# The order table of a fused RWKV-6 and Hyena kernel, searched anew

## The chip, the cores and the metric

The kernel runs on one core of a Trainium2 chip. The core has five engines that each work through a queue of their own in order: TensorE (PE, whose weight loads are shown apart as PEld), VectorE (DVE), ScalarE (ACT), GpSimd (POOL) and SyncE (SP, which here only issues DMAs). The metric is the device time of one execution in microseconds, lower is better; the time before is a median of 3 runs.

## The reference, cut to what matters

Two stages. The first is a recurrence over 768 time steps for each of 4 batches and 8 heads of width 48; the second takes its output as 4 sequences of 768 tokens and 384 channels.

```python
def _attn_ref(r, k, v, w, u):                 # each [4, 8, 768, 48]
    for t in range(S):
        cur = np.einsum('bhd,bhe->bhde', u[None] * kt, vt)
        y[:, :, t] = np.einsum('bhd,bhde->bhe', rt, state + cur)
        state = wt[:, :, :, None] * state + np.einsum('bhd,bhe->bhde', kt, vt)

def _moe_ref(x, w_proj, filter_fft, w_out):   # x [4, 768, 384]
    x1, x2, x3 = split(x @ w_proj)
    x2_conv = np.fft.irfft(np.fft.rfft(x2, axis=1) * np.fft.rfft(filter_fft, axis=0)[None], axis=1)
    return (x1 * x2_conv * x3) @ w_out
```

## The kernel before, in words

**First stage.** Each sequence of 768 steps is cut into 6 chunks of 128, and two chunks are treated as a pair, so there are 12 pairs (`group(gi, i0)` and `pair(i0, gi)`, with i0 = 0, 2, ... 22). A pair's four inputs come by one 384 KB DMA each: `lw`, `lk`, `lr`, `lv`. Then, for pair number gi and its chunks i:

- `wm` multiplies neighbouring decays, `ln` (ACT) takes the logarithm, `cs` (PE) sums it up, `ex` (ACT) takes the exponential, and `kq` (DVE, one per chunk) scales keys and receptances with it into a bf16 tile `kq`. `tr` (PE) transposes that, `qk` (ACT, one per chunk) evicts it, `sc` (PE) makes the scores.
- The scores are evicted and cut by a mask into the tile `mt`, in one of three ways: one DVE multiplication for both halves (written `M` in the table), one DVE multiplication per half (`mt i.a D`), or an ACT copy (`A`) and a POOL multiplication behind it (`mc i.a G`).
- `rk`, `ru`, `rh`, `cc`, `vc` make the term with u: a product of r and k, times u, an addition of the two halves of each row (`rh`), a sum along the row (`cc`, over 24 elements if `rh` ran and over 48 if it did not, written `M`), and a product with v in bf16 (`vb` is the cast of v).
- `ki` and `kv` (PE) and `su` (DVE) carry the state; `yi`, `ys`, `y` (PE) make the output of the pair, `xn` (ACT) evicts it, `yt` (PE) and `xT` transpose it for the second stage.

**Second stage**, once per batch b, as soon as its 6 chunks are there: `p` and `q` project x to x1 and x3 (L1561) with evictions `cp` and `cq` (`cq` multiplies both), `xw` projects to x2 (L1601) with `cxw`; `sd` adds and subtracts halves of the sequence, `f` is the forward transform as matmuls (L1458) with `cf`; `u`, `p` without numbers of halves (DVE, L1638) multiply with the filter's spectrum; `E` is the inverse transform (L1656), `cE` and `aE` evict it, and `yE` multiplies with the gate. An `E` with the letter `Q` writes a folded form in matmuls of half the width, which two more additions `dE` on DVE or POOL unfold; with `P` there are no such additions. `o` projects out (L1720), `co` evicts, `so` stores. The filter's own spectrum is made once: three DMAs `filt`, two DVE operations `fsd` (L1521), then `h`, `hc`, `hg`.

**Start.** `ang`, `ia` (DVE) and `sin`, `is` (ACT) make the transform's matrices; `if` flips some of them. ACT holds one table of functions at a time; a row `table` loads another.

**What sets the order.** Each operation is registered with `plan.op(...)`, and the string `ORDER` (line 45 on) says line by line which comes next, on which engine, and in which of the 8 PSUM banks it writes. `Plan.run` emits them in that order, so an engine's queue is the sequence of its own rows. Waits between engines follow from the tiles that are read and written. A third word that names a DVE operation is a tie: the instruction waits until that operation has ended. `warm` and `spare` are matmuls on zeros (512 or 128 columns) that fill PE's idle time. A helper records most elementwise work, so many groups of the profile have the lines L1104 (a product) or L1108 (an ACT copy).

```python
            o = self.ops.pop(name)
            if o.one or o.two:
                place[(o.one + o.two)[0]] = int(more[0])
            got = o.fns[e](e, place)
            if more and got is not None and more[0] in last:
                tie(got, last[more[0]])
```

Of the kernel before, what the change touches and what calls it, by code (L numbers as in the profile page):

```python
# [271 lines left out]
wm4 D
vb3 A
yt3 P 2
ru4 D
yt5 P 7
lr10 S
qk6 A
xT3 D
kv6 P  # L280
vc3 G wm4
rh4 -
cc4 M
xT5 A
qk7 A
xw0.4 P 6
lv8 S
cxw0.0 A
su6 D
rk6 D  # L290
ln4 A
sc6 P 4
sc7 P 0
lw10 S
cxw0.4 A
xw0.2 P 2
mt6.0 M
kw6 G su6
cs8 P 6
lr14 S  # L300
cxw0.2 A
mt7.0 M
p0.0.1 P 4
sd0.0.0 D
p0.0.0 P 0
cp0.0.1 A
ru6 D
p0.2.0 P 4
sd0.1.0 D
lk14 S  # L310
cp0.0.0 A
ki7 P 5
q0.0.1 P 2
rk5 D
cp0.2.0 A
lv10 S
ex8 A
rh6 D
kv7 P
cq0.0.1 D  # L320
wm6 G rk5
vb4 A
f0.0 P 0
lw14 S
kq9 D
vc4 G rk5
f0.1 P 2
cf0.0 A
su7 D
kq8 D  # L330
f0.2 P 0
cf0.1 A
wm5 G
lv16 S
cc6 D
tr8 P 2
cf0.2 A
ru5 D
kw5 D
yi6 P 4  # L340
lr16 S
qk9 A
ys7 P
qk8 A
# [7 lines left out]
u10.0 D  # L352
ph8 A
sc8 P 0
lv12 S
xn7 A
q0.0.0 P 6
xn6 A
u00.0 D
mt8.0 N  # L360
lw16 S
ki8 P 3
kv8 P
# [44 lines left out]
vb8 A
cq0.2.1 D
cs12 P 0  # L410
kq11 D
p1.0.0 P 4
ph10 A
cE0.1 A
wm8 G
ex12 A
aE0.1.0 D
lk18 S
tr10 P 6
kw7 G  # L420
aE0.1.1 D
cp1.0.0 A
kq12 D
xw1.0 P 2
qk10 A
vb6 A
kq13 D
q1.0.0 P 4
lw20 S
qk11 A  # L430
vc6 G
rh5 -
cc5 M
lv18 S
ph12 A
cxw1.0 A
tr12 P 6
lr18 S
cq1.0.0 D
sc11 P 0  # L440
qk12 A
p1.2.0 P 2
vc5 G
qk13 A
mt11.0 M
ki10 P 4
kv10 P
cp1.2.0 A
lr20 S
sc10 P 5  # L450
ln8 A
ki12 P 7
mt10.0 M
yt9 P 3
wm9 G
E0.0 Q 0
xT9 A
sc12 P 2
cE0.0 A
rk8 G  # L460
su10 D
kv12 P
yi10 P 5
vb7 A
aE0.0.1 D
ys10 P
ys11 P
mt12.1 D
mt12.0 A
mc10.0 -  # L470
mt10.1 -
mc10.1 -
mc11.0 -
mt11.1 -
mc11.1 -
y10 P
lv22 S
aE0.0.0 D
lv20 S
cs14 P 2  # L480
xn11 A
mc12.0 G
su12 D
xn10 A
sc13 P 0
yt11 P 4
ex14 A
mt13.0 M
yt10 P 5
kw8 G  # L490
E0.2 P 6
xT10 A
xT11 A
# [1322 lines left out]
```

## Time and profile before

| | |
|---|---|
| median of 3 runs | 157.8 us (157.19 to 158.36) |
| the profiled execution | 158.33 us, of which 156.6 us are the span of the profile |
| busy | PE 143.6 us, DVE 143.2, ACT 111.9, POOL 93.0 |
| PE's matmuls on zeros, in the first 60 us | 19.35 us |
| read and written | 22.41 MB and 4.72 MB |

The span runs from the first to the last instruction of the profiled execution. Of the 22.41 MB most are the inputs of the pairs, which are read in the first 85 us. The pairs and the second stage of the batches overlap: the filter's spectrum is made at about 27 to 34 us, the second stage of the first batch starts at about 40 us, and the last 20 us hold the second stage of the last batch alone.

### The profile page before, as it was taken

What the parts mean: (1) busy time and instruction counts of PE and PEld (TensorE: products, weight loads), DVE (VectorE), ACT (ScalarE), POOL (GpSimd) and SP (SyncE); (2) the same over time, 40 slices, a digit from 0 to 9 for tenths busy, and PEclk for the clock granted to TensorE, in tenths of its full rate; (3) what the DMA queues carried; (4) which work ended last, traced back from release to release, by engine and by line L of the source; (5) the groups of instructions that cost most, each with busy time, mean ns of one, the idle gap of its engine ahead of it and who ended that gap; (6) DMA issues with size and microseconds to landing.
All of it is one profiled execution on the core that took longest, in us unless ns stands there. A gap on an engine that the chain in (4) does not pass through costs nothing.

```text
span 156.6 us, 5491 instructions
## 1 busy us (share of the span) xinstructions
PE 143.6 (92%) x2321; PEld 88.3 (56%) x2321; DVE 143.2 (91%) x245; ACT 111.9 (71%) x202; POOL 93.0 (59%) x85
## 2 busy tenths in 40 slices
PE   6888997898999999989999898999999999999990
PEld 2243544465755557547656674676656767556650
DVE  6999999999999999899999899799899997799860
ACT  3595976858787788798787596896764597654561
POOL 6915493659271729959959776793779527400300
PEclk9999999999999999999999999999999999999999
DMA  4999999999999999399797300510000050000665
GB/s 120 315 303 305 272 236 306 374 257 251 284 274 262 285 293 273 102 249 255 189 259 181 60 4 0 207 73 34 0 4 0 4 201 4 0 0 4 249 261 193
DMA packets 53770, 27.19 MB, mean 174 GB/s; under 512 B 50289, under 2 KB 52210, under 8 KB 53746
## 3 DMA queue, kind: packets, MB, share of 16 engines
q1 hardware_dynamic: 53346, 26.55, 59.2%
q0 software_dynamic: 400, 0.29, 1.4%
q8 instruction: 18, 0.29, 0.8%
q14 instruction: 6, 0.05, 0.1%
HBM read 22.41 MB, written 4.72 MB: 173 GB/s over the span
## 4 chain that ended last, share of the span: by engine, by line
PE 55%; DVE 23%; ACT 11%; issue 6%; POOL 2%; ACTq 1%; POOLq 0%; DVEq 0%
PE banks L1561 11%; PE banks L1720 8%; PE banks L1601 7%; PE banks L1458 6%; DVE kq L1287 5%; PE banks L1656 4%; PE banks L1322 3%; DVE P L1521 2%; PE banks L1365 2%; DVE cc L1259 2%; PE banks L1391 2%; PE banks L1400 2%; PE banks L1423 2%; DVE mt L1332 2%; ACT qk L1108 2%
## 5 line engine op out<-in xcount | busy, mean ns | idle before, releaser
L1561 PE MATMUL banks<-xT,wproj 128*128 128x384 bf16 x144 | 28.3, 326 | 0.0
L1332 DVE TENSOR_TENSOR mt<-banks,mask_cut 128x1024 bf16<-128x1024 f32 (+1 forms) x22 | 24.8, 1142 | 0.9 <-PE banks L1322 0.8
L1104 POOL TENSOR_TENSOR vc<-vb,cc 128x768 bf16<-128x768 bf16 x12 | 18.3, 1525 | 10.7 <-ACT vb L1108 7.2
L1108 ACT ACTIVATE x<-banks 128x768 bf16<-128x768 f32 (+1 forms) x28 | 19.6, 714 | 5.8 <-PE banks L1601 3.8
L1287 DVE TENSOR_TENSOR kq<-banks,kr 128x768 bf16<-128x768 f32 x24 | 22.1, 946 | 0.2
L1104 POOL TENSOR_TENSOR kr<-kr,w 128x768 f32<-128x768 f32 x7 | 13.9, 1990 | 6.8 <-DMA w<-in_w_dram 2.1
L1561 PEld LDWEIGHTS <-wproj 128*128 128x128 bf16 x144 | 13.0, 97 | 8.2 <-issue 0.7
L1160 PE MATMUL banks<-wt 128*128 128x512 bf16 x61 | 17.2, 426 | 0.0
L1108 ACT ACTIVATE X<-banks 128x768 bf16<-128x768 f32 x12 | 9.8, 813 | 7.8 <-PE banks L1458 7.7
L1601 PE MATMUL banks<-wproj,xT 128*128 128x384 bf16 x72 | 14.1, 327 | 1.0 <-ACT xT L1108 0.8
L1104 POOL TENSOR_TENSOR rk<-kr 128x768 bf16<-128x768 f32 x7 | 14.3, 2043 | 0.3 <-DVE g L1589 0.2
L1108 ACT ACTIVATE qk<-banks 128x512 f32<-128x512 f32 x24 | 13.6, 602 | 1.3 <-PE banks L1301 1.3
L1104 POOL TENSOR_TENSOR y<-y,g 128x768 bf16<-128x768 bf16 (+1 forms) x5 | 6.7, 1351 | 12.8 <-DVE y L1682 12.4
L1589 DVE TENSOR_TENSOR g<-banks,x 128x768 bf16<-128x768 f32 (+1 forms) x16 | 12.7, 802 | 1.2 <-ACT qk L1108 1.2
L1458 PE MATMUL banks<-sd,F 128*128 128x384 bf16 (+1 forms) x96 | 13.5, 328 | 0.0
L1337 POOL TENSOR_TENSOR mt<-mt,mask_cut 128x512 bf16<-128x512 bf16 (+1 forms) x5 | 7.9, 1590 | 8.9 <-ACT mt L1108 8.9
L1720 PE MATMUL banks<-wout,y 128*128 128x384 bf16 x72 | 13.2, 326 | 0.0
L1108 ACT ACTIVATE xn<-banks 128x384 bf16<-128x384 f32 x24 | 10.6, 492 | 3.5 <-PE banks L1391 3.1
L1104 POOL TENSOR_TENSOR wp<-w 128x384 f32<-128x384 f32 x11 | 11.1, 1006 | 3.2 <-PE banks L1561 3.2
L1108 ACT ACTIVATE o<-banks 128x768 f32<-128x768 f32 (+1 forms) x14 | 9.5, 697 | 4.2 <-PE banks L1720 4.0
L1458 PEld LDWEIGHTS <-F 128*128 128x128 bf16 (+1 forms) x120 | 8.6, 103 | 6.6 <-issue 2.5
L1104 POOL TENSOR_TENSOR rk<-rk,u_b 128x768 bf16<-128x768 bf16 x4 | 6.9, 1736 | 8.6 <-DVE rk L1104 4.9
(115 smaller groups left out, 326.7 us busy)
## 6 DMA issues: line engine op xcount, KB each, us to landing
w<-in_w_dram SPq DMA_DIRECT2D x12, 384.0 KB, 5.1
kr<-in_k_dram SPq DMA_DIRECT2D x12, 384.0 KB, 5.3
kr<-in_r_dram SPq DMA_DIRECT2D x12, 384.0 KB, 5.7
v<-in_v_dram SPq DMA_DIRECT2D x12, 384.0 KB, 5.3
out_dram<-o SPq DMA_DIRECT2D x9, 384.0 KB, 2.8
x<-in_moe_w_proj_dram SPq DMA_DIRECT2D x2, 576.0 KB, 7.3
out_dram<-o SPq DMA_DIRECT2D x6, 192.0 KB, 1.9
U<-in_moe_filter_fft_dram SPq DMA_DIRECT2D x2, 384.0 KB, 7.1
```

The source lines that it names most:

```text
L1104: return eng(e).tensor_mul(o, a, b)
L1108: return nc.scalar.activation(out=o, in_=a, func=AF.Copy)
L1160: nc.tensor.matmul(banks[:, at, :].rearrange("p (a t) -> p a t", a=2), wt[:, 0:L], _mid(wt, 2), start=True, stop=True)
L1287: op(f"kq{i0 + a}", [DVE], lambda e, bk, a=a: nc.vector.tensor_mul(kq[fs[a]][:, :, :, 0:D], csp(bk)[:, :, 0:C].rearrange("p m (h d) -> p m ...
L1332: return copy(ACT, o, x) if e in (ACT, ACT2) else nc.vector.tensor_mul(o, x, _mid(mask_cut[:, c], n))
L1337: return nc.gpsimd.tensor_mul(o, o, _mid(mask_cut[:, c], n))
L1458: nc.tensor.matmul(p[rows], F[:, ti, c0 + rows.start:c0 + rows.stop], x[q][:, ti, :], start=(ti == 0), stop=(ti == NT - 1),)
L1561: nc.tensor.matmul(p, wproj[:, cb, col0:col0 + L], xT[bx][:, cb, sl], start=(cb == 0), stop=(cb == CB - 1),)
L1589: op("c" + n3, [DVE], lambda e, bk: nc.vector.tensor_mul(g[bx][:, fs, sl].rearrange("p f (t a) -> p f a t", a=2), halved(view(bk, n3)), ha ...
L1601: nc.tensor.matmul(view(bk)[:, z], xT[bx][:, cb, (c0 + z) * L:(c0 + z + 1) * L], wproj[:, cb, C:2 * C], start=(cb == 0), stop=(cb == CB - 1),)
L1656: nc.tensor.matmul(o, P[:, q, m, cs], x, start=start, stop=stop)
L1720: nc.tensor.matmul(view(bk)[:, z], yt_[:, z, :], wout[:, cb, :], start=(cb == 0), stop=(cb == CB - 1),)
```

## The change

Only the string `ORDER` is another one; the code that builds operations is the same. The new table has the same operations. Their order differs in nearly every stretch, by a few places mostly, and so do banks. Apart from order and banks it changes these choices (before, then now; `-` means that the operation is left out or done with its neighbour):

```
start       kz1, kz3, rk1: DVE -> POOL      wm1, ru1, rk2: POOL -> DVE
            rh0, rh1: - -> POOL, tied       cc0, cc1: over 48 (M) -> over 24 (D)
            mt0.0, mt0.1: one DVE product (M) -> ACT copy with POOL product mc0.0, and DVE product
            ACT's tables: 4 loads -> 6 loads
to 65 us    mt4: M -> two DVE products      xT3: DVE -> ACT       wproj1: POOL -> ACT
            rh4, cc4: -, M -> D, D          rh6, cc6: D, D -> -, M
            rk5: DVE -> POOL, tied to sd0.1.0
later       mt8: one ACT copy and one POOL product -> two of each
            vb5: ACT -> POOL   rh5: - -> POOL, cc5: M -> D   rk10: POOL -> DVE
            E0.0: Q with dE0.0.0 and dE0.0.1 on POOL -> P
            xT12, xT21, xT23, cp2.2.1, co3.1: DVE -> ACT     cE2.1: ACT -> DVE
            rh9, cc9: -, M -> D, D    rh11: - -> POOL, tied; cc11: M -> D
            mt16: its two halves change engines
            dE1.1.1, yE2.1, yE3.0.0: POOL -> DVE
            dE2.2.0, sd3.1.2, yE3.0.1, yE3.2.1: DVE -> POOL
zero work   warm 61 -> 79 (50 of them ahead of the first tr), spare 15 -> 13
```

Three lines of the diff show the form:

```diff
-rk5 D
+rk5 G sd0.1.0
...
-E0.0 Q 0
+E0.0 P 4
```

**ACT's queue at the start.** Before, from the second table load to the first eviction `qk` of the first pair and on to the logarithm of the third pair (lg is the logarithm's tile, banks the sums of `cs`, F and mi the transform's matrices):

```order
L987 ACT_TABLE_LOAD
L1235 ACTIVATE lg_75<-wp_65 128x8x48
L1235 ACTIVATE lg_74<-wp_64 128x8x48
L1283 ACTIVATE banks<-banks 128x2x384 x2
L1108 ACTIVATE vb_83<-v_70 128x768
L1290 ACTIVATE phi<-banks 128x8
L1108 ACTIVATE qk_96<-banks 128x512
L1108 ACTIVATE qk_95<-banks 128x512
L987 ACT_TABLE_LOAD
L1471 ACTIVATE F<-o_127,mpi 128x768
L1471 ACTIVATE F<-o_128,mpi 128x768
L987 ACT_TABLE_LOAD
```

Now, the same stretch from its second table load to the fifth (mt_99 is the first half of the scores of chunk 0):

```order
L986 ACT_TABLE_LOAD
L1470 ACTIVATE mi<-X,mpi 128x6x192
L986 ACT_TABLE_LOAD
L1282 ACTIVATE banks<-banks 128x2x384
L1234 ACTIVATE lg_75<-wp_65 128x8x48
L1107 ACTIVATE vb_83<-v_70 128x768
L1289 ACTIVATE phi<-banks 128x8
L1107 ACTIVATE qk_96<-banks 128x512
L1107 ACTIVATE qk_95<-banks 128x512
L1234 ACTIVATE lg_76<-wp_64 128x8x48
L1282 ACTIVATE banks<-banks 128x2x384
L986 ACT_TABLE_LOAD
```

Two loads more stand in the queue, around the sine `mi`, which stood ahead of the second load before; the exponential of the second pair (L1282) has moved behind the evictions `qk` of the first.

**DVE ahead of the filter.** Before, from the state of chunk 0 (S_104) to the scores of chunk 3 (P<-U is `fsd`):

```order
L1371 TENSOR_TENSOR S_104<-banks,phi 128x384
L1332 TENSOR_TENSOR mt_99<-banks,mask_cut 128x1024
L1259 TENSOR_REDUCE cc_80<-rk_77 128x16
L1332 TENSOR_TENSOR mt_100<-banks,mask_cut 128x1024
L1371 TENSOR_TENSOR S_105<-banks,phi 128x384
L1521 TENSOR_TENSOR P<-U 128x1152
L1104 TENSOR_TENSOR rk_79<-rk_79,u_b 128x768
L1521 TENSOR_TENSOR P<-U 128x1152
L1332 TENSOR_TENSOR mt_102<-banks,mask_cut 128x1024
L1287 TENSOR_TENSOR kq_91<-banks,kr_68 128x16x48
L1287 TENSOR_TENSOR kq_90<-banks,kr_68 128x16x48
```

Now, the same stretch:

```order
L1370 TENSOR_TENSOR S_104<-banks,phi 128x384
L1286 TENSOR_TENSOR kq_92<-banks,kr_67 128x16x48
L1370 TENSOR_TENSOR S_105<-banks,phi 128x384
L1258 TENSOR_REDUCE cc_81<-rk_78 128x16
L1286 TENSOR_TENSOR kq_93<-banks,kr_67 128x16x48
L1331 TENSOR_TENSOR mt_99<-banks,mask_cut 128x512
L1520 TENSOR_TENSOR P<-U 128x1152 x2
L1103 TENSOR_TENSOR rk_79<-rk_79,u_b 128x768
L1286 TENSOR_TENSOR kq_91<-banks,kr_68 128x16x48
L1286 TENSOR_TENSOR kq_90<-banks,kr_68 128x16x48
L1331 TENSOR_TENSOR mt_102<-banks,mask_cut 128x1024
```

The two `fsd` now follow each other directly, only one half of mt_99 is left on DVE, and the scores of chunk 3 (mt_102) have moved behind the third pair's two `kq`.

**DVE where the first batch's second stage begins** (sd are the sums and differences, g a gate). Before:

```order
L1371 TENSOR_TENSOR S_106<-banks,phi 128x384
L1104 TENSOR_TENSOR rk_77<-kr_68 128x768
L1332 TENSOR_TENSOR mt_101<-banks,mask_cut 128x1024
L1332 TENSOR_TENSOR mt_102<-banks,mask_cut 128x1024
L1612 TENSOR_TENSOR sd<-x_114 128x1152
L1104 TENSOR_TENSOR rk_77<-rk_77,u_b 128x768
L1612 TENSOR_TENSOR sd<-x_114 128x1152
L1104 TENSOR_TENSOR rk_79<-kr_67 128x768
L1256 TENSOR_TENSOR rk_77<-rk_77 128x16x24
L1589 TENSOR_TENSOR g_111<-banks,x_110 128x2x2x192
```

Now:

```order
L1103 TENSOR_TENSOR rk_77<-kr_68 128x768
L1103 TENSOR_TENSOR rk_77<-rk_77,u_b 128x768
L1370 TENSOR_TENSOR S_106<-banks,phi 128x384
L1331 TENSOR_TENSOR mt_101<-banks,mask_cut 128x1024
L1331 TENSOR_TENSOR mt_102<-banks,mask_cut 128x1024
L1611 TENSOR_TENSOR sd<-x_114 128x1152 x2
L1258 TENSOR_REDUCE cc_81<-rk_78 128x16
L1286 TENSOR_TENSOR kq_90<-banks,kr_66 128x16x48
L1370 TENSOR_TENSOR S_103<-banks,phi 128x384
```

The product `rk5` (rk_79<-kr_67) has left DVE's queue for POOL's, the two `sd` stand together, and `cc4` (cc_81) has come in behind them.

1155 lines of the change are left out of this document (577 added, 578 removed).

## The prediction

> **What bounds the kernel now.** The page's first two parts come first: which engine is full, and when.
>
> ```profile
> PE 143.6 (92%) x2321; PEld 88.3 (56%) x2321; DVE 143.2 (91%) x245; ACT 111.9 (71%) x202; POOL 93.0 (59%) x85
> PE   6888997898999999989999898999999999999990
> DVE  6999999999999999899999899799899997799860
> ```
>
> Two engines are full at once. PE's digits of the first third contain matmuls on zeros, so the view of stretches says more (columns: PE, PEld, DVE, ACT, POOL busy, clock, DMA share, GB/s), with the tile of zeros alone beneath.
>
> ```profile
> 4.00:65.00 61.00, 56.06 (x940) 32.50 (x937) 60.32 (x101) 46.19 (x79) 36.66 (x30) 1.00 1.02 281
> 26.80:65.00 38.20, 36.32 (x681) 23.10 (x680) 37.86 (x55) 29.87 (x56) 23.89 (x16) 1.00 1.00 278
> 65.00:150.00 85.00, 82.51 (x1365) 53.51 (x1364) 79.03 (x125) 62.07 (x117) 53.59 (x38) 1.00 0.32 94
> 150.00:156.60 6.60, 2.44 (x15) 1.27 (x13) 1.32 (x3) 2.35 (x5) 0.00 (x0) 1.00 0.66 238
> ...
> 26.80:60.00 33.20, 2.61 (x18) 1.22 (x18) 0.00 (x0) 1.00 1.03 286
> ```
>
> From 4 to 65 us DVE is busy 60.32 of 61 us: there it is the bound. PE has room there: from 26.8 to 65 us 38.2 - 36.32 + 2.61 of zeros = 4.5 us. From 65 to 150 us it turns round: PE idles 85 - 82.51 = 2.49 us, DVE 5.97, and the last 6.6 us are copies and stores. So DVE work taken out before 65 us counts in full, PE work added after 65 us counts in full, DVE work after that counts little.
>
> **Prices.** Groups with shapes apart (out<-in, count, busy us, mean ns):
>
> ```profile
> L1332 DVE TENSOR_TENSOR mt<-banks,mask_cut 128x1024 bf16<-128x1024 f32 x19 | 22.8, 1216 | 0.9 <-PE banks L1322 0.8
> L1332 DVE TENSOR_TENSOR mt<-banks,mask_cut 128x512 bf16<-128x512 f32 x3 | 2.0, 679 | 0.0
> L1259 DVE TENSOR_REDUCE cc<-rk 128x16 f32<-128x768 bf16 x10 | 9.4, 941 | 0.0
> L1259 DVE TENSOR_REDUCE cc<-rk 128x16 f32<-128x384 bf16 x2 | 1.1, 541 | 0.0
> L1256 DVE TENSOR_TENSOR rk<-rk 128x384 bf16<-128x384 bf16 x2 | 0.7, 346 | 0.0
> L1104 DVE TENSOR_TENSOR rk<-kr 128x768 bf16<-128x768 f32 x5 | 4.8, 951 | 0.0
> L1104 DVE TENSOR_TENSOR rk<-rk,u_b 128x768 bf16<-128x768 bf16 x8 | 4.4, 544 | 0.0
> L1104 DVE TENSOR_TENSOR wp<-w 128x384 f32<-128x384 f32 x1 | 0.6, 550 | 0.0
> L1195 DVE MEMSET kq<- 128x128 uint32 x3 | 0.5, 165 | 0.0
> L1110 DVE COPY xT<-banks 128x384 bf16<-128x384 bf16 x4 | 1.4, 350 | 0.2 <-PE banks L1423 0.2
> L987 ACT ACT_TABLE_LOAD x4 | 5.1, 1283 | 0.8 <-PEq L1800 0.8
> L1108 ACT ACTIVATE mt<-banks 128x512 bf16<-128x512 f32 x3 | 1.8, 592 | 0.5 <-PE banks L1322 0.5
> L1656 PE MATMUL banks<-mi,P 128*128 128x384 bf16 x42 | 7.7, 326 | 0.0
> L1656 PE MATMUL banks<-mi,P 128*128 128x192 bf16 x20 | 2.5, 246 | 0.0
> ```
>
> **The start, up to the end of the filter's `fsd`.** DVE loses kz1 and kz3 (2 x 0.165), rk1 (0.951), the full mt0 (1.216) and two long sums cc (2 x 0.941): 4.38 us. It gains ru1 (0.544), wm1 (0.550), rk2 (0.951), half an mt (0.679) and two short sums (2 x 0.541): 3.81. That is 0.57 less. Two more rows count here, and both come from DVE's and POOL's timelines and the list of DMAs (start, us; the last row is the issue whose landing time stands above it):
>
> ```profile
> 9.14 0.96 DVE L1104 TENSOR_TENSOR rk<-kr 128x768 bf16<-128x768 f32 x1
> 22.54 2.52 DVE L1521 TENSOR_TENSOR P<-U 128x1152 bf16<-128x1152 f32 x1
> 25.45 1.35 DVE L1521 TENSOR_TENSOR P<-U 128x1152 bf16<-128x1152 f32 x1
> ...
> 22.37 1.48 POOL L1104 TENSOR_TENSOR vc<-vb,cc 128x768 bf16<-128x768 bf16 x1
> ...
> kr<-in_r_dram SPq DMA_DIRECT2D x1, 384.0 KB, 4.4
> 4.14 0.38 SPq L1229 DMA_DIRECT2D kr<-in_r_dram  x1
> ```
>
> The first fsd takes 2.52 us and the second, of equal size, 1.35. POOL's vc began 0.17 us ahead of the first and ended at 23.85, and the fsd ended 1.2 us later: it stood behind vc. Now vc0 comes earlier and rk3 is tied behind the second fsd, so 1.17 us go. Against that, rk0 needs the load lr0. Before it was the fourth large load and landed at 4.14 + 4.4 = 8.5 us; now it is the fifth. With 281 GB/s in the row of the first stretch, 384 KB take 1.4 us, so it lands at about 9.9 (an estimate), where DVE started rk0 at 9.14: 0.8 us of waiting. DVE would so be 0.57 + 1.17 - 0.8 = 0.9 us early behind the filter.
>
> I do not count it, because of ACT. Chunk 3's scores mt3.0 have moved behind kq4, and they wait for `sc3`, that for `qk2`, and in ACT's queue qk2 now stands behind mt0.0, ex4, both xn, vb1 and xT0; and ACT has two table loads more. The added ACT work is 2 x 1.283 + 0.592 = 3.16 us. What covers it are ACT's own waits there:
>
> ```profile
> 13.84 0.84 ACT L1108 ACTIVATE vb<-v 128x768 bf16<-128x768 f32 x1 [1.14 <-DMA v<-in_v_dram]
> 22.45 0.52 ACT L1235 ACTIVATE lg<-wp 128x384 bf16<-128x384 f32 x1 [1.03 <-POOL wp L1104]
> 25.17 0.49 ACT L1108 ACTIVATE xn<-banks 128x384 bf16<-128x384 f32 x1 [1.16 <-PE banks L1391]
> 28.03 0.81 ACT L1527 ACTIVATE hh<-banks 128x768 bf16<-128x768 f32 x1 [0.93 <-PE banks L1458]
> ```
>
> Together 4.26 us of waiting, so the 3.16 fit, but with little over, and ACT is then full up to qk2. Those 0.9 us are what I expect mt3.0 to wait. **Start: 0**, with the bounds -0.9 (ACT covered) and +2.3 (3.16 bare, less 0.9).
>
> How long a table switch holds ACT is read here:
>
> ```profile
> 8.73 1.28 ACT L987 ACT_TABLE_LOAD   x1
> 10.02 0.94 ACT L1235 ACTIVATE lg<-wp 128x384 bf16<-128x384 f32 x2
> ```
>
> The load ends at 10.01 and the logarithm starts at 10.02. [...]
>
> **From there to 65 us, on DVE.** xT3 goes (0.350), rk5 goes (0.951); mt4 in halves adds 2 x 0.679 - 1.216 = 0.14; rh4 with the short cc4 is 0.346 + 0.541 - 0.941 = -0.05, and cc6 the reverse. **-1.16 us**, on the engine that is the bound, and PE with its 4.5 us of room can follow. rk5 on POOL is tied behind the first sd, and vc4 stands behind it; POOL is busy 36.66 of 61 us there, and its work hides unless yi6 waits for vc4. Between -1.16 and 0 (PE not following) I take all of it: nothing else in that stretch is full.
>
> **After 65 us.** E0.0 without folding: four matmuls of 192 columns become 384, 4 x (326 - 246) = **+0.32 us** on PE, which is the bound there. The two additions dE0.0 leave POOL, where they waited for nothing that PE needs soon. On DVE rk10 comes in (0.951), three xT go (1.05), and cc5 and cc11 get short (0.80); the copies and small products that are swapped with ACT and POOL besides are of about half a microsecond each and more leave than come. That is some 0.9 us less, but DVE has 5.97 us idle there: 0 for the end, and at best all of PE's 2.49 idle us. ACT takes the copies; it is busy 62.07 of 85 us. co3.1 on ACT falls in the last 6.6 us, in which ACT is busy 2.35: 0. The loads have nearly all landed by then (share 0.32). The zeros behind the filter are of about equal number in both tables, and those ahead of it fill PE's waits: 0.
>
> **Sum:** 0 - 1.16 + 0.32 = -0.84 us. The profiled execution took 158.33 us (span 156.6), so 157.5 for it; that execution lies 0.53 above the median of 157.8, so **157.0 us** as a median. A measurement of this kernel can tell about 1%, 1.6 us, from no change: the forecast is within it.
>
> **Rivals.**
>
> *ACT becomes the bound of the start (slower).* One mechanism: the table loads, six now, that stand ahead of the exponentials of the first and third pair. The point from which it decides: qk2's eviction ends after DVE has finished kq4, and PE's y0 and h wait for ACT too. For it: the added 3.16 us against 4.26 of cover, and lr0's later landing moves the whole chain of the first pair. Against: 1.14 of the cover is a wait for lv0, the eighth large load in both tables. Price: 3.16 bare, -0.84 + 3.16 = +2.3, **160.1 us**.
>
> *POOL and DVE block each other more often (slower).* The row of fsd shows the price: 1.17 us for one meeting. POOL newly gets rk1, rh0, rh1, mc0.0, rk5, rh5, rh11, dE2.2.0, sd3.1.2 and a part of yE3. Most of them are tied to the end of a DVE operation, but rk1, mc0.0, rh5 and yE3.0.1 are not. Three meetings on the path: 3.5 - 0.84 = +2.7, **160.5 us**. [...]
>
> *The gain reaches further (faster).* ACT covers the start (-0.9), and PE's waits after 65 us are halved (-1.25), since DVE has 0.9 us less to do there and xT copies no longer stand in its queue: -0.84 - 0.9 - 1.25 = -3.0, **154.8 us**.
>
> *The relief does not arrive (no change).* If PE, not DVE, sets the pace already from 27 us on, the -1.16 are lost and E0.0 costs 0.32: **158.1 us**.
>
> **How the numbers follow.** The forecast 0.30, the relief that does not arrive 0.12: both within 1%, together 0.42. The faster rival 0.28. ACT at the start 0.18, the blocking 0.12: slower, together 0.30. The two tables are the same in structure, and no stretch is rebuilt, which keeps the ends near. The range leaves out the outer half of the faster rival and the outer third of the slower ones: 154.8 to 160.2 us.
>
> **What would show it.** The first fsd at about 1.35 us and not 2.52. rk0 starting at 9.8 to 10, with a wait for the load or a long `ang0` before it. mt3.0 on DVE with a wait of up to 1 us for PE behind qk2. The first batch's product P (L1638), before at 61.2 us, at about 60. PE's idle time between 65 and 150 us near 2.5 us. The prediction is wrong if ACT is seen full from 18 to 33 us with DVE waiting for more than 1 us, if DVE's products of two SBUF tiles grow well beyond the means above, or if PE's idle time in the later half moves by more than 1.5 us either way.

## The result, and the profile after

The changed kernel takes **162.88 us** (median of 3 runs, 162.41 to 163.74) against 157.8: a ratio of **1.033, 95% interval 1.024 to 1.042**. The prediction was 157.0 with a range up to 160.2. The profiled execution took 162.41 us, its span is 160.7 us, 4.1 more than before.

The page of the kernel after, parts 1 and 2 in extract (busy us; granted clock in tenths):

```profile
PE 147.2 (92%) x2337; PEld 89.4 (56%) x2337; DVE 145.4 (90%) x241; ACT 117.0 (73%) x211; POOL 94.0 (59%) x90
...
PEclk9999999999699999999999999999999999999998
```

DVE has four instructions fewer than before and yet 2.2 us more of busy time, and TensorE's clock falls once, in the eleventh slice (40 to 44 us). The view of stretches (PE, PEld, DVE, ACT, POOL busy; clock; DMA share; GB/s) places the loss:

```profile
4.00:65.00 61.00, 53.51 (x850) 29.97 (x850) 57.22 (x85) 45.38 (x73) 32.60 (x30) 0.97 0.88 243
65.00:150.00 85.00, 83.89 (x1453) 54.68 (x1446) 81.35 (x123) 65.11 (x128) 55.82 (x40) 1.00 0.40 112
...
35.00:40.00 5.00, 2.21 (x62) 1.61 (x61) 4.87 (x9) 2.46 (x3) 1.90 (x2) 0.97 1.09 295
40.00:45.00 5.00, 5.00 (x88) 2.73 (x86) 3.90 (x6) 3.42 (x6) 2.36 (x2) 0.69 1.15 317
```

In the first 65 us DVE gets through 85 instructions where it got through 101. After 65 us the new table is better than the old one: PE idles 85 - 83.89 = 1.1 us instead of 2.5. The first batch's product `P` (the wide one, on U) is the mark between the two; before it started at 61.15, now at 67.98:

```profile
67.98 1.34 DVE L1637 TENSOR_TENSOR P<-U 128x2304 bf16<-128x2304 bf16 x1
```

So 6.8 us are lost ahead of `P` between these two executions, and behind it the span is 160.7 - 67.98 = 92.7 us long instead of 156.6 - 61.15 = 95.45, which is 2.7 shorter. Where the 6.8 us go is seen in DVE's timeline of the kernel after (start, us; hh is the filter's spectrum, made by `hg`), with POOL's beneath:

```profile
32.26 0.25 DVE L1532 COPY hh<-hh 128x384 bf16<-128x384 bf16 x1
32.42 0.55 DVE L1536 TENSOR_SCALAR hh<-banks 128x384 bf16<-128x384 f32 x1
32.89 0.90 DVE L1103 TENSOR_TENSOR rk<-rk,u_b 128x768 bf16<-128x768 bf16 x1
33.71 1.53 DVE L1532 COPY hh<-hh 128x384 bf16<-128x384 bf16 x1
35.27 1.74 DVE L1534 COPY hh<-hh 1x384 bf16<-1x384 bf16 x1
```

```profile
32.34 1.03 POOL L1103 TENSOR_TENSOR wp<-w 128x384 f32<-128x384 f32 x1 [1.31 <-DMA w<-in_w_dram]
33.33 1.79 POOL L1103 TENSOR_TENSOR vc<-vb,cc 128x768 bf16<-128x768 bf16 x1
35.08 1.82 POOL L1103 TENSOR_TENSOR kr<-kr,w 128x768 f32<-128x768 f32 x1
```

The same two copies in the kernel before:

```profile
31.08 0.24 DVE L1533 COPY hh<-hh 128x384 bf16<-128x384 bf16 x1
31.36 0.25 DVE L1535 COPY hh<-hh 1x384 bf16<-1x384 bf16 x1
```

A quarter of a microsecond each before; now 1.53 and 1.74, each ending with the POOL product beside it (33.33 + 1.79 = 35.12; 35.08 + 1.82 = 36.90). Together with the product `rk` ahead of them (0.90 for 0.55) that is 3.1 us. PE waits 2.81 us for the same `hg`, and then runs cold: the clock of 0.69 from 40 to 45 us above. PE's timeline of the kernel after:

```profile
37.78 0.41 PE L1321 MATMUL banks<-qk 48*64 48x128 bf16 x14 [2.81 <-DVE hh L1536]
...
40.77 2.31 PE L1159 MATMUL banks<-wt 128*128 128x512 bf16 x5
```

Five products on zeros take 2.31 us, where the same five take 1.25 in the run with early `kq1` below, and DVE waits another 1.05 us for PE at 43.5. Nearer the start, an operation on the angles and the first of the flips `if` are long beside POOL's work too (DVE first, then POOL):

```profile
7.89 2.62 DVE L1482 TENSOR_SCALAR X<-o,fcol 128x192 int32<-128x192 f32 x1
...
17.12 0.98 DVE L1499 TENSOR_SCALAR mi<-mi,sgn 128x384 bf16<-128x384 bf16 x1
```

```profile
7.71 1.93 POOL L1103 TENSOR_TENSOR rk<-kr 128x768 bf16<-128x768 f32 x1
9.59 0.80 POOL L1194 MEMSET kq<- 128x256 bf16 x3
...
17.07 0.91 POOL L1255 TENSOR_TENSOR rk<-rk 128x384 bf16<-128x384 bf16 x1
```

The angle's operation ends at 10.51, the three MEMSETs behind POOL's `rk1` at 10.39; `if` ends at 18.10 and `rh1` at 17.98. The other operations on the angles beside it (L1479, L1482) take 0.30 to 0.56, and `if` took 0.31 before. This is the meeting of POOL and DVE that the prediction held for unlikely. Long in the rows above are not only a product of two SBUF tiles (`rk`, 0.90 us) but also plain copies (1.53 and 1.74) and operations with a scalar (2.62 and 0.98).

**Why the meetings happen.** The table ties exactly these POOL instructions: `rh1 G if`, `vc0 G if`, `wm3 G hg0`, `vc2 G hg0`. But POOL starts `rh1` at 17.07, ahead of `if`, and `wm3` and `vc2` at 32.34 and 33.33, ahead of `hg0`. The instruction lists show that the tie is not there. Rows of POOL's list in the kernel after, and of the kernel with the repair below, with what each instruction waits for:

```
after     32 L1255 TENSOR_TENSOR rk_78<-rk_78 128x16x24
repaired  32 L1255 TENSOR_TENSOR rk_78<-rk_78 128x16x24 [waits DVE_49]
after     38 L1103 TENSOR_TENSOR wp_65<-w_61 128x384 [waits DMAHW5_49]
repaired  38 L1103 TENSOR_TENSOR wp_65<-w_61 128x384 [waits DMAHW5_49,DVE_49]
```

`Plan.run` remembers the last instruction of an operation only if its function returns one, and makes a tie only to an operation that it remembers. The functions behind `if` (`flips`) and `hg0` (`gcopy`) return nothing. No tie of the old table names them, and all its 19 ties reach the program; 4 of the 25 ties of the new table do, and they are dropped without a word. The two waits above are all that the repair adds to POOL's list: `vc0` waits for the later `cc0` anyway, and `vc2` stands behind `wm3`.

### The profile page after: what moved, and what is told of

Same layout as the page of the kernel before. It is cut to its first block, busy times and chain, and to the rows that moved or that the text cites. A ratio compares the mean times of both kernels' runs of the same rounds, so it can differ in the third digit from the quotient of the medians.

```text
span 160.7 us, 5528 instructions
## 1 busy us (share of the span) xinstructions
PE 147.2 (92%) x2337; PEld 89.4 (56%) x2337; DVE 145.4 (90%) x241; ACT 117.0 (73%) x211; POOL 94.0 (59%) x90
## 4 chain that ended last, share of the span: by engine, by line
PE 58%; DVE 19%; DMA 8%; issue 4%; ACT 4%; SPq 3%; POOL 1%; ACTq 0%; DVEq 0%
PE banks L1560 13%; PE banks L1457 8%; DMA w<-in_w_dram 7%; PE banks L1655 7%; PE banks L1600 6%; PE banks L1719 5%; DVE kq L1286 4%; SPq L1228 3%; PE banks L1321 3%; PE banks L1300 3%; PE banks L1422 3%; PE banks L1390 3%; DVE X L1482 2%; PE banks L1364 2%; PE banks L1399 2%
## 5 line engine op out<-in xcount | busy, mean ns | idle before, releaser
L1560 PE MATMUL banks<-xT,wproj 128*128 128x384 bf16 x144 | 27.6, 326 | 0.0
L1159 PE MATMUL banks<-wt 128*128 128x512 bf16 x79 | 22.0, 428 | 1.1 <-DVE wt L1192 1.1
L1103 POOL TENSOR_TENSOR kr<-kr,w 128x768 f32<-128x768 f32 x7 | 13.1, 1874 | 8.3 <-DVE rk L1103 8.3
L1103 POOL TENSOR_TENSOR rk<-kr 128x768 bf16<-128x768 f32 x7 | 13.5, 1922 | 5.9 <-DVE P L1520 3.0
L1321 PE MATMUL banks<-qk 48*64 48x128 bf16 x384 | 10.9, 221 | 3.3 <-DVE hh L1536 2.8
L1159 PEld LDWEIGHTS <-wt 128*128 128x128 bf16 x79 | 7.8, 106 | 10.9 <-issue 3.8
L1336 POOL TENSOR_TENSOR mt<-mt,mask_cut 128x512 bf16<-128x512 bf16 (+1 forms) x7 | 9.1, 1302 | 8.1 <-ACT mt L1107 7.9
L1588 DVE TENSOR_TENSOR g<-banks,x 128x768 bf16<-128x768 f32 (+1 forms) x16 | 12.8, 804 | 0.1
L1107 ACT ACTIVATE o<-banks 128x768 f32<-128x768 f32 (+1 forms) x15 | 10.0, 682 | 3.6 <-PE banks L1719 3.5
L1103 POOL TENSOR_TENSOR wp<-w 128x384 f32<-128x384 f32 x10 | 10.4, 1036 | 3.1 <-issue 1.7
L1103 POOL TENSOR_TENSOR y<-y,g 128x384 bf16<-128x384 bf16 (+1 forms) x5 | 6.1, 1229 | 10.0 <-DVE y L1681 8.2
```

The lines of the kernel that those rows point to most:

```text
L1103: return eng(e).tensor_mul(o, a, b)
L1107: return nc.scalar.activation(out=o, in_=a, func=AF.Copy)
L1159: nc.tensor.matmul(banks[:, at, :].rearrange("p (a t) -> p a t", a=2), wt[:, 0:L], _mid(wt, 2), start=True, stop=True)
L1321: nc.tensor.matmul(p[rz[z], par, j, :], x[d, j, rz[c]], x[d, HP + j, :], start=True, stop=True)
L1560: nc.tensor.matmul(p, wproj[:, cb, col0:col0 + L], xT[bx][:, cb, sl], start=(cb == 0), stop=(cb == CB - 1),)
L1588: op("c" + n3, [DVE], lambda e, bk: nc.vector.tensor_mul(g[bx][:, fs, sl].rearrange("p f (t a) -> p f a t", a=2), halved(view(bk, n3)), ha ...
```

## The experiments

The kernel before took 157.17 to 157.22 us (medians) beside these runs. Differences in microseconds below are the difference of two ratios times 157.2. The changed kernel stands at 1.033, that is +5.2 us.

### The dead ties

**Both functions return their instruction.**

```diff
-            eng(e).tensor_scalar(out=mi[:, 2, :, 1, :], ...
+            return eng(e).tensor_scalar(out=mi[:, 2, :, 1, :], ...
...
-                nc.vector.tensor_scalar(
+                return nc.vector.tensor_scalar(
```

> The new table unchanged; only the two recorded functions of `if` and `hg` now hand back their last DVE instruction, so that the four ties to `if` and `hg0` (rh1, vc0, wm3, vc2) reach POOL's queue. Theory 1, dead ties: in the profile of the new table the operations of hg0 took 1.53 and 1.74 us instead of 0.24 and 0.25 while POOL ran vc2 and kw3, and the first of `if` 0.98 instead of 0.31 while POOL ran rh1: 3.4 us of DVE; PE then stood still for 2.81 us and its clock fell to 0.69 in the stretch from 40 to 45 us. With the ties those rows go back to their usual length, the clock stays near 1.0, and the time falls by 3.4 to 5 us, to 158 to 159.5. Rival, the order itself is slow and the blocking is hidden: vc2 and kw3 come later instead, 162 to 163.

Measured: 157.99 us, ratio **1.0063 [1.0031, 1.0095]**. The copies are back at 0.25 (DVE's timeline of this kernel), and POOL waits for them:

```profile
34.44 0.26 DVE L1532 COPY hh<-hh 128x384 bf16<-128x384 bf16 x1
34.73 0.25 DVE L1534 COPY hh<-hh 1x384 bf16<-1x384 bf16 x1
```

```profile
35.79 1.00 POOL L1103 TENSOR_TENSOR wp<-w 128x384 f32<-128x384 f32 x1 [3.67 <-DVE hh L1536]
```

The dead ties cost 1.033 - 1.006 = 2.7%, 4.2 us (by the two intervals, 4.2 with 1.5 either way). What is left, +1.0 us, is still not the forecast of -0.8.

**Only the tie to `hg0`.**

```diff
-                nc.vector.tensor_scalar(
+                return nc.vector.tensor_scalar(
```

> As the run with both ties, but only `hg` hands its instruction back: the ties of wm3 and vc2 hold, those of rh1 and vc0 to `if` are still dead. Theory 1: nearly all of the gain is here, since 2.8 of the 3.4 us and PE's standstill are at hg0: 158.5 to 160. Rival, the start decides (rk0 at 11.28 us, `if` stretched by 0.67): most of the loss stays, 161.5 to 163.

Measured: 158.35 us, 1.0060 [1.0030, 1.0091]: the same as with both. The ties to `if` are worth nothing at the end, though with them `if` takes 0.31 instead of 0.97.

**Zeros against the cold clock, ties left dead.**

```diff
-warm 4 7
+warm 18 7
```

> The new table with its dead ties; 18 matmuls on zeros instead of 4 ahead of sc2, which fill the 2.81 us in which PE stood still there. Theory 1: DVE's blocked copies stay at 1.5 and 1.7 us, so mt2.0 starts as late as before (38.7 us); only the clock's fall in 40 to 45 us goes, and with it the stretched zeros (5 in 2.31 us) ahead of sc5, some 1.2 us: 161 to 162. Rival, the clock's fall is most of the loss: 159 to 160. If the clock has no part: 162.9.

Measured: 161.33 us, 1.0254 [1.0214, 1.0294], with `P` at 66.60. The copies are still held (0.61 and 1.87, and 1.35 for the product between them; the POOL products beside them take 0.99 to 2.13), the clock is full (1.00 from 35 to 45 us). By the two ratios the fallen clock is some 1.2 of the 4.2 us and the blocking itself 3.0. The intervals of these ratios overlap, but the times do not (160.97 to 162.19 against 162.41 to 163.74), and the profiled executions, neither of them with a fallen clock before 35 us, lie 1.3 apart (161.07 and 162.41).

**The old table with one tie taken away.**

```diff
-vc2 G ru3
+vc2 G
```

> The kernel before with one word less: vc2 on POOL is no longer tied to ru3, so that it can start as soon as cc2 and vb2 are there, in the middle of hg. Theory 1: vc2 (1.48 us) runs beside the copies of hg, which wait for it; DVE comes 0.5 to 1.5 us later there, and the time goes to 158.2 to 159.3. Rival, blocking at this place is covered: 157.8, no change.

Measured: the profiled execution took 157.98 us, with one copy of `hg` held for 1.19 us instead of 0.24 (to 31.10, where POOL's `vc2` ends at 30.98); the three timed ones took 162.17 to 162.92, at a granted clock of 0.963 to 0.975 instead of 0.998. The executions fall into two groups, so no ratio is given. The meeting is shown: take the live tie away and the copy is held in the old table too. Its price is not: the execution that was profiled is 0.8 us above the kernel before, and what made the other three long is open, since none of them left a profile.

### Which part of the new table is good

The two tables hold the same operations, so one can be cut behind an operation and go on in the other's order. All have the ties alive.

**Old table up to `hg1` (31 us), then new.** The first rows change and the rest stays as in the repaired kernel:

```diff
-u S
-lk2 S
...
+ki0 P 6
...
 hg1 D
```

> The old table up to and with `hg1` (31 us in the old profile), then every operation that is left in the new table's order, with the new table's engines and ties. Theory 1 (the new table's start is its bad part, and its part behind it is the better one): the first product of the gates, `P`, stays near 61 us, and the part behind it keeps the 1.2 to 2.7 us that the new table's profiles show from there to the end: 155.0 to 156.5. Theory 2 (the new table's later part is not better; it only runs faster there because it comes late, with its loads and PE work in stock): 157.2 or above, to 159.

Measured: **156.09 us, 0.9924 [0.9910, 0.9939]**, faster than both kernels. `P` starts at 61.59, and 154.3 - 61.59 = 92.7 us follow it, as in the kernel after.

**Old table up to `ln4` (45 us), then new.**

```diff
 ln4 A
-sc6 P 4
-sc7 P 0
+xw0.2 P 1
```

> The old table up to and with `ln4` (some 45 us in the old profile, nothing left over from ahead of the cut), then the new table's order. Theory 1: nearly as with the earlier cut, 155.5 to 156.7, since DVE's cheaper products of the chunk loop lie behind 45 us in part only. Theory 2: 157.2 to 158. If only the earlier cut gains, what gains lies between 31 and 45 us.

Measured: 156.28 us, 0.9946 [0.9931, 0.9962]. `P` at 61.60, 93.0 us behind it.

**New table up to `sc5`, then old.**

```diff
 sc5 P 5
-yt3 P 7
 wproj0 A
-cs6 P 1
```

> The other half alone: the new table with its ties alive up to and with `sc5`, then the old table's order. Theory 1 (the new start is bad, the new later part good): slower than the repaired table, since the late start is kept and the gain is lost: 159 to 161. Theory 2 (the later part is neither better nor worse): 158.0 within 0.5.

Measured: 162.01 us, 1.032 [1.025, 1.039]; slower than expected. `P` at 64.69, and 95.6 us behind it, as in the old table. That the repaired table has `P` at 64.76 is chance: its profiled execution had a cold TensorE at the start (see below) and came to the scores `mt3.0` at 31.35, this one at 30.09. So from there to `P` this hybrid takes 1.2 us longer (34.60 against 33.41); that cost of the joint is in its 162.01.

| profiled execution | `P` starts | to the second `P` | from there to the end of the span |
|---|---|---|---|
| before | 61.15 | 47.3 | 48.1 |
| after | 67.98 | 46.1 | 46.6 |
| new, ties alive | 64.76 | 46.1 | 46.6 |
| old start to `hg1`, then new | 61.59 | 46.1 | 46.6 |
| new start to `sc5`, then old | 64.69 | 47.3 | 48.3 |

Both halves show: the new start is late, the part behind `P` is 2.7 us shorter, 1.2 of it ahead of the second batch's `P` and 1.5 behind. The hybrid gains only 1.2 us on the old kernel, because the new order between 31 us and `P` takes some of it back: with the old table up to 84 and 115 us (below) `P` starts at 60.0 and 60.4, not at 61.6. (The profiled execution of before, 158.33 us, is one of its longer ones, so its 61.15 is late.) DVE's timeline of the hybrid cut at `hg1`, and PE's, show the place:

```profile
46.37 1.23 DVE L1330 TENSOR_TENSOR mt<-banks,mask_cut 128x1024 bf16<-128x1024 f32 x1 [1.54 <-PE banks L1320]
```

```profile
41.41 0.51 PE L1421 MATMUL banks<-ident,xn 128*128 128x128 bf16 x6 [0.62 <-ACT xn L1106]
...
45.83 0.42 PE L1320 MATMUL banks<-qk 48*64 48x128 bf16 x16 [0.53 <-ACT x L1106]
```

DVE stands 1.54 us for PE, which stands for ACT's evictions. Of the 1.54 us PE's own waits for ACT are 0.62 and 0.53. In the old table DVE came to these scores at 45.37 without a wait.

**Old table up to `lv20` (84 us), and up to `sc18` (115 us), then new.**

```diff
 lv20 S
+wout G
+lk20 S
+ln9 A
```

```diff
+xw2.4 P 4
 mt18.0 M
-xw2.4 P 2
 mc19.1 G
```

> The old table up to and with `lv20` (about 84 us in the old profile, nothing left over), then the new table. If what the new table gains are PE's waits (of the old profile's eight waits behind `P`, 2.3 us in all, six with 1.8 us lie behind 84 us): 156.2 to 156.7. If the gain lies between 61 and 84 us, where DVE's work got less: 157.0 to 157.4.

> The old table up to and with `sc18` (about 115 us in the old profile, nothing left over), then the new table. Two of the eight waits (0.4 us) lie behind that. If the gain are PE's waits, spread: 156.8 to 157.2. If it lies at the end of the span (ACT takes one more copy of the output, PE's last products come in another order): 156.0 to 156.5.

Measured: 156.7 us, 0.9974 [0.9958, 0.9990], and **155.96 us, 0.9920 [0.9902, 0.9938]**. The later cut holds the whole gain of the hybrid cut at `hg1`. The second batch's `P` shows why, first in that hybrid, then in the one cut at `sc18`, which has the old order up to there:

```profile
107.70 1.35 DVE L1636 TENSOR_TENSOR P<-U 128x2304 bf16<-128x2304 bf16 x1
```

```profile
107.73 1.35 DVE L1638 TENSOR_TENSOR P<-U 128x2304 bf16<-128x2304 bf16 x1
```

What the new order loses between 31 us and the first `P` it has won back by the second, and no more (the second execution is one of 156.38, 0.4 above its median); all that it gains at the end lies behind 108 us. What a joint costs comes on top, as the cut at `lv20` shows with its 156.7. (With the earlier one PE has two waits that neither table has, 0.42 and 1.00 us.) The stretches from the second `P` to the third and from there to the end, before:

```profile
108.47:127.06 18.59, 18.22 (x348) 11.96 (x345) 17.79 (x24) 12.28 (x24) 11.71 (x8) 1.00 0.01 2
127.06:156.60 29.54, 25.11 (x207) 15.37 (x202) 21.80 (x47) 17.31 (x30) 7.41 (x6) 1.00 0.32 121
```

and with the new table from `sc18` on:

```profile
107.73:125.54 17.81, 17.81 (x336) 11.80 (x335) 17.34 (x25) 13.18 (x26) 11.79 (x8) 1.00 0.07 24
125.54:154.70 29.16, 25.33 (x226) 15.28 (x215) 20.86 (x43) 17.60 (x32) 8.75 (x8) 0.98 0.29 109
```

0.78 and 0.38 us shorter, and PE's idle time falls by 0.37 and by 4.43 - 3.83 = 0.60: most of the gain here is PE's waiting.

### What makes the new start late

With the ties alive, the new start costs 1.0063 - 0.9924 = 1.4%, 2.2 us. Each run below takes one suspect away.

**`rk1` on DVE, so that it holds no angle.**

```diff
-rk1 G
...
+rk1 D
 ru1 D
```

> The changed kernel with all four ties alive, and `rk1` moved from POOL to DVE, just ahead of `ru1`. Theory 1 (what the repaired table still loses is lost at its start, where the untied `rk1` on POOL blocks a DVE copy of the FFT's angles for 2.7 us): the blocked copy goes back to about 0.4, `rk0` starts when `lr0` lands, at 9.9 to 10.2 instead of 11.2; `rk1` itself costs DVE 0.95. Net on the end 0.3 to 1.3 us less than with the ties alone: 156.7 to 157.7. Theory 2 (the start is not what the end waits for, since what is lost there is caught up): 158.0 within 0.4.

Measured: 158.05 us, 1.0059 [1.0030, 1.0088]. The angle's operation is short again (0.69), and `rk0` waits 0.52 for its load and starts at 10.01, as the prediction had worked out. But `P` stays at 64.7: the 0.95 us of `rk1` on DVE, and PE's standstill behind it, took its place.

**Zeros for PE's standstill ahead of `tr0`.**

```diff
-warm 31 5
+warm 40 5
```

> The changed kernel with all ties alive and `rk1` on DVE, where `warm 31 5` ahead of `tr0` becomes `warm 40 5`: nine more products on zeros (0.22 us each) fill the 2.06 us for which PE stands there. If the fall of the granted clock behind that standstill is what makes the start late, clock 1.0 from 17 to 25 us, DVE's wait for `sc1` 0.3 to 0.6 us shorter, and the time 0.5 us or more lower: under 157.6. If the lateness is that of DVE's order alone, 157.8 to 158.2.

Measured: 158.27 us (158.08 to 158.63), 1.0070 [1.0054, 1.0086]. The clock is full (1.00 from 4 to 30 us), `P` is at 63.8 and DVE's wait for `sc1` 0.87 instead of 1.09, but the median is no better. The run before it tells why: of its 10 executions three show a clock of 0.989 and 158.9 to 159.5 us, the others 0.997 to 1.0 and 157.6 to 158.3. The repaired table has the same two groups (4 of 10 at 0.989, 159.2 us), and its profiled execution, one of the long ones, shows where the clock falls (PE's timeline, then the view of stretches):

```profile
17.26 0.80 PE L1300 MATMUL banks<-ident,kq 64*128 64x64 bf16 x32 [2.19 <-DVE kq L1286]
```

```profile
17.00:20.00 3.00, 2.74 (x49) 1.37 (x53) 2.30 (x7) 2.07 (x5) 1.98 (x3) 0.72 1.13 283
```

In the profiled execution of the changed kernel PE stood 2.12 us at the same place and the clock stayed at 1.00. With the zeros none of 4 executions is long, which by itself could be luck at three or four in ten; they also delay `tr0`, to 17.76 from 17.14. PE's cold stretch is worth about 1.3 us, in some executions only.

**The first products `kq1` and `kq0` ahead of work in stock.**

```diff
 rk0 D
+wm1 D
+kw0 D
...
-rk1 D
-ru1 D
-kw0 D
...
 kq0 D
+rk1 D
+ru1 D
+kw1 D
```

> The changed kernel with all ties alive and `rk1` on DVE, and at the start the first chunks' products `kq1` and `kq0`, for which PE waits, put ahead of `rk1`, `ru1` and `kw1`; `rh0` and `wm2` are tied to `ru0`. Theory 1 (the new start is late because DVE makes work in stock ahead of `kq1` and `kq0`, so that PE stands for 2 us, goes cold, and DVE then waits for PE): the first transposition `tr0` at about 15 us instead of 17.1, DVE's wait for `sc1` (1.1 us) under 0.4, the end of the filter's two `fsd` 1.0 to 1.8 us earlier than 28.4, the gates' first product `P` at 62.8 to 63.8 instead of 64.7; time 156.3 to 157.2. Theory 2 (the lateness comes from the order behind 17 us): `P` at 64.3 or later, 157.7 to 158.3.

Measured: 157.89 us, 1.0067 [1.0028, 1.0105]. The step did what it says (`tr0` at 15.33, no wait for `sc1`, the two `fsd` done at 27.1 instead of 28.4), and `P` did not move (65.0). PE's timeline of this run shows what came instead, with DVE's wait for the scores `mt3.0` behind it:

```profile
21.43 0.32 PE L1353 MATMUL banks<-S,ident 128*128 128x384 bf16 x1 [1.85 <-DVE S L1370]
...
22.28 3.44 PE L1159 MATMUL banks<-wt 128*128 128x512 bf16 x8
```

```profile
31.62 1.23 DVE L1331 TENSOR_TENSOR mt<-banks,mask_cut 128x1024 bf16<-128x1024 f32 x1 [1.63 <-PE banks L1321]
```

**That standstill filled as well.**

```diff
-warm 7 5
+warm 16 5
 ki1 P 2
```

> The kernel with the early `kq1` and `kq0`, and `warm 7 5` ahead of `ki1` made `warm 16 5`, which fills the 1.85 us for which PE stood there; after that standstill the next eight products on zeros took 3.44 us instead of 1.7, ahead of `tr2`. If the clock's fall is what kept the early products from helping: `tr2` at about 24.1 us instead of 25.65, the gates' product `P` at 63.4 to 64.0 instead of 65.0, time 156.8 to 157.5. If what holds the start is ACT's queue ahead of `qk2`: DVE's wait for the scores `mt3.0` is still over 1 us, `P` at 64.3 or later, 157.6 to 158.1.

Measured: 158.07 us, 1.0045 [1.0023, 1.0067]. In the profiled execution (157.41, the shortest of 6) `P` is at 63.0; yet the median lies where the second answer put it. The long group of the run before (4 of 10 at 0.989) is gone, here and in the two runs below that keep these zeros and do not make PE stand elsewhere: none of 20 executions is below 0.994. So it is PE's standstill that makes it.

**`qk2` early in ACT's queue**, on that kernel and on the plain repaired table:

```diff
+qk2 A
 xn0 A
...
-qk2 A
 rk3 G fsd1
```

> As the one before, and in ACT's queue `qk2` ahead of both `xn`, `ph2`, `vb1` and `xT0`. If ACT's queue holds the start (the prediction's first rival): `mt3.0` waits under 0.4 us, `P` 1 us or more earlier than without this step, 156.2 to 157.0. If the loss lies in the order behind 31 us: `P` moves by less than 0.4, 157.4 to 158.0.

> The changed kernel with all four ties alive, and `qk2` alone moved ahead of both `xn`, `ph2`, `vb1` and `xT0` in ACT's queue. If ACT's queue holds the start, also where DVE is late itself: `mt3.0` starts without its wait of 0.6 us, and the time is 0.4 to 0.7 us below that of the ties alone: 157.3 to 157.6. If not: 158.0 within 0.3, or more, since `xn` and with it the first projections come 0.6 us later.

Measured: 159.25 us, 1.0133 [1.0086, 1.0180], and 159.05 us (158.41 to 161.12; 1.0106 [1.0064, 1.0148] without the longest of the four): both slower, and DVE waits longer, here in the first, where it had waited 0.62 without this step:

```profile
31.99 1.23 DVE L1331 TENSOR_TENSOR mt<-banks,mask_cut 128x1024 bf16<-128x1024 f32 x1 [2.71 <-PE banks L1321]
```

Two queues meet ahead of `mt3.0`. In the changed kernel (ACT's timeline, then PE's) the eviction `qk2` ends at 29.55, the filter's `h1` runs from 28.62 to 29.79, and `sc3` starts at 29.72:

```profile
28.96 0.59 ACT L1107 ACTIVATE qk<-banks 128x512 f32<-128x512 f32 x1
```

```profile
28.62 1.17 PE L1457 MATMUL banks<-P,F 128*64 128x384 bf16 x12
29.72 0.42 PE L1321 MATMUL banks<-qk 48*64 48x128 bf16 x16
```

So neither queue alone could bring `mt3.0` forward by more than 0.2 us: in PE's queue of the new table `sc3` stands behind `yt0`, which waits for `xn0`, and behind `h1`. `qk2` early made `xn0` late instead, some 0.5 us, and PE stood 1.61 us for it and not 1.12. Behind that the clock fell to 0.59 (28 to 32 us): the zeros of `spare` took 1.51 us for 0.89 and `h1` 2.00 for 1.17, which is most of the longer wait:

```profile
27.77 1.51 PE L1164 MATMUL banks<-wt 128*128 128x128 bf16 x13 [1.61 <-ACT xn L1107]
```

**`sc3` ahead of `yt0` in PE's queue**, again on both:

```diff
+sc3 P 6
 spare 13 2
 yt0 P 2
...
-sc3 P 6
```

> The kernel with the early first products, the filled standstill and `qk2` early, and now also `sc3` ahead of `yt0` and of the filter's `h1` in PE's queue, as the old table has it. If PE's queue was what `mt3.0` stood behind: its wait on DVE falls from 2.71 us to under 0.3, `P` from 65.4 to about 62.5 to 63, and the time from 159.25 to 156.8 to 157.6. If not, `mt3.0` still waits over 1 us and the time stays above 158.

> The changed kernel with all four ties alive, `qk2` early and `sc3` ahead of `yt0` in PE's queue. If PE's queue was what `mt3.0` stood behind: no wait at `mt3.0` (2.64 with `qk2` early alone, 0.61 with the ties alone), and a time of 157.2 to 157.8, below the 158.0 of the ties alone; the late first products and the cold stretch are still in it. If not: 158.3 or more.

Measured: 158.08 us, 1.0049 [1.0036, 1.0062], and 158.66 us, 1.0094 [1.0063, 1.0124]. The wait at `mt3.0` is gone in both; the second's row:

```profile
28.78 1.21 DVE L1331 TENSOR_TENSOR mt<-banks,mask_cut 128x1024 bf16<-128x1024 f32 x1
```

That settles what `mt3.0` waited for, both queues at once, and not the time: neither run is better than the ties alone by more than the noise.

**Pair 0 loaded first**, with `wm1` and the flips of `if` ahead of `kq1`:

```diff
-lk2 S
+lk0 S
...
-lr2 S
+lr0 S
...
 ru0 D
+wm1 D
+if D
+rh0 G if
+wm2 G if
...
-if D
```

> The kernel with early first products, filled standstill, and `qk2` and `sc3` early; now `lk0` and `lr0` are loaded ahead of `lk2` and `lr2`, and `wm1` and the `if` products stand between `ru0` and `kq1`, with `rh0` and `wm2` tied to `if`. If the late loads are what is left of the start's loss: `rk0` at 9.3 to 9.5 instead of 9.80, no wait for the decay's load, the scores `mt3.0` and `P` 0.5 to 0.8 us earlier (`P` at 62.3 to 62.6), time 157.2 to 157.6 instead of 158.1. If not: `P` moves by less than 0.3, 157.9 to 158.3, and what is left stays open.

Measured: 157.80 us, 1.0044 [1.0027, 1.0061], `P` at 63.2: not the 0.5 us expected. `rk0` starts at 9.38 without a wait, and DVE has no wait from there to 46 us, but a product later takes 1.66 us beside POOL's `rh1`, which runs from 16.57 to 18.13, and gives the time back (0.95 in the changed kernel, at 18.64):

```profile
17.28 1.66 DVE L1103 TENSOR_TENSOR rk<-kr 128x768 bf16<-128x768 f32 x1
```

So the new start's 2.2 us have no single cause. Five are shown at work in the timelines: `rk1` (as a block or as 0.95 us on DVE), pair 0's late loads, the late `tr0` with PE cold in some executions, `sc3` behind `qk2` and `h1`, and further meetings with POOL. None of the nine runs brings the end forward by more than 0.3 us, which is within the noise of the ties alone; that each cause has another close behind it is what this suggests, and is not shown. The cold stretch, 1.3 us in 4 of 10 executions, is some 0.5 us of the mean. How the rest splits stays open.

## Why the prediction was wrong, and where it was right

The terms, with what the runs put in their place:

| term | forecast | measured | from |
|---|---|---|---|
| start | 0 (-0.9 to +2.3) | +2.2 | ties alive against the hybrid cut at `hg1` |
| 31 us to the end | -1.16 + 0.32 = -0.84 | -1.2 | that hybrid against the kernel before |
| POOL and DVE block each other | 0 (a rival, +3.5, chance 0.12) | +4.2 | dead ties, 1.2 of it the clock |
| sum | -0.84 | +5.2 | |

The last column closes by construction, since each row is the difference of two runs next to each other; what a joint of two tables costs is inside the first two rows.

**The step that failed** is the blocking rival: "Most of them are tied to the end of a DVE operation, but rk1, mc0.0, rh5 and yE3.0.1 are not". The mechanism and the price of a meeting were there (1.17 from the row of `fsd`; here 1.3 and 1.5 on the copies of `hg`), and three meetings on the path is what came, 3.1 us for the 3.5; that TensorE cools behind them, 1.2 us more, it did not have. The rival also looked only at what POOL newly gets. The three that met `hg`, `wm3`, `vc2` and `kw3`, had been on POOL before; what changed for them is that `vc2` lost its live tie to `ru3` for a dead one to `hg0`, and that `wm3`, which had stood behind it, now comes ahead of it. What was wrong is the reading that a tie in the table is a tie in the program. The line of `Plan.run` that makes it also has the condition `more[0] in last`; whether `if` and `hg0` ever get into `last` was a matter of two functions' ends, and POOL's instruction list, read with its waits, would have shown it. One of the untied it named, `rk1`, also met DVE (2.62 for 0.3 to 0.6), and moving it changed nothing at the end.

**Start.** Its single readings held. The `fsd`, which took 2.52 and 1.35 before, take 1.31 each:

```profile
24.83 2.62 DVE L1520 TENSOR_TENSOR P<-U 128x1152 bf16<-128x1152 f32 x2
```

Once `rk1` is out of the way, `rk0` waits for `lr0` and starts at 9.8 to 10.4 in six runs, where 9.8 to 10 was worked out. `mt3.0` waited 0.61, within "up to 1 us". Its cause, "that for `qk2`", was half of it: `qk2` early made the wait 2.71, and only with `sc3` moved in PE's queue as well was it gone. From 18 to 33 us ACT is busy 13.15 of 15 us, not full, and removing that wait did not bring the end forward. So the first rival (ACT becomes the bound of the start) had nearly its price, +2.3 for +2.2, and not its mechanism. The term is mis-sized: 0 stood for +2.2. What the sum lacked is the order itself, as far as is known: what DVE makes ahead of `kq1`, for which PE stands 2 us, and the clock behind that; the larger part is open.

A table load of the new start holds ACT for its own 1.28 us too, where ACT has work to go on with: behind three of the six in the changed kernel the next operation starts within 0.02 us. One in ACT's timeline of the run with early `kq1` (the load ends at 12.00, the exponential starts at 12.01):

```profile
10.72 1.28 ACT L986 ACT_TABLE_LOAD   x1
12.01 0.80 ACT L1282 ACTIVATE banks<-banks 128x768 f32<-128x768 f32 x1
```

**From there to 65 us.** The -1.16 did not reach the end. DVE has less to do, but waits 1.54 us for PE at 46 us, and `P` comes 1.2 to 1.6 us later than with the old order there: against -1.16, +1.2 to +1.6. The step that failed here is "PE with its 4.5 us of room can follow": the room was there as a sum, and not ahead of the products that DVE waited for. The rival "the relief does not arrive" was right on this term.

**After 65 us.** Against +0.32 the part behind `P` is 2.7 us shorter. (E0.0 itself is small: behind the first `P` the 72 products of the inverse transform keep PE busy for 12.8 us in the hybrid cut at `hg1` and for 12.7 before.) "The gain reaches further" had the right mechanism for half of it, "PE's waits after 65 us are halved (-1.25)". The view of PE's waits behind 61 us (us in total, times, longest), before:

```profile
PE banks L1601 <- ACT xT L1108: 0.5, 2, 0.3
PE banks L1322 <- ACT qk L1108: 0.5, 1, 0.5
PE banks L1301 <- ACT x L1108: 0.4, 1, 0.4
PE banks L1301 <- ACT qk L1108: 0.3, 1, 0.3
PE banks L1601 <- DVE y L1682: 0.2, 1, 0.2
PE banks L1322 <- ACT X L1108: 0.2, 1, 0.2
PE banks L1322 <- DVE mt L1332: 0.2, 1, 0.2
```

and in the hybrid cut at `hg1`:

```profile
PE banks L1421 <- ACT xn L1106: 0.6, 1, 0.6
PE banks L1599 <- ACT xT L1106: 0.4, 1, 0.4
```

2.3 us became 1.0, so 1.3 of the 2.7. In all, the view of stretches has PE idle 95.45 - 88.79 = 6.66 us behind `P` before and 92.71 - 87.83 = 4.88 in the hybrid, 1.8 less; the other 1.0 is busy time of PE, not taken apart here. That the two errors nearly cancel, so that -0.84 stands against -1.2, is luck.

## What to carry to other kernels

An order that is only wished for, here a tie in a table, is read in the emitted instructions with their waits and not in the table; a name that is not found should be an error. Where GpSimd and VectorE share work, look at the short copies between SBUF tiles on the critical path: here those of 0.25 us that met a GpSimd product ended with it, at 1.53 and 1.74, and the standstill was paid again, 1.2 us, when TensorE cooled. And when a searched order loses, cut it: old up to a point, new from there, and the good part shows itself (155.96 us here, against 157.2 and 162.9).

## What the runs showed of the hardware that was not expected

A copy of one partition was held no less than one of 128: the 1x384 bf16 took 1.74 us for 0.25, beside a POOL product of 1.82, and the 128x384 bf16 ahead of it 1.53 for 0.24, beside one of 1.79. And the clock fell behind short standstills of PE: behind 2.81 us the granted clock was 0.69 from 40 to 45 us, behind 2.19 us it was 0.72 from 17 to 20 us (the start of the repaired table, where 4 of 10 executions are long), behind 1.61 us 0.59 from 28 to 32 us (`qk2` early). Yet behind 2.12 us in the changed kernel it stayed at 1.00, from 17 to 20 us as well, so the length alone does not decide; what else does is not shown here.
